# Modulation gradient sums gathered in shared PSUM rows, output column sums behind filler, w_mod rows dealt among the pairs

## The chip, the cores and the metric

The kernel runs on one core of a Trainium2 chip. The metric is the device time of one execution in microseconds (us). Before the change it is 1656.85 us (median of 3 runs, 1653.53 to 1657.62). Engines: PE is TensorE, PEld its weight loads, DVE VectorE, ACT ScalarE, POOL GpSimd, SP SyncE; SPq is SyncE's queue, where the shown time is the issuing of a transfer. The lines of the profile name tiles: pg, pu, pcs, pv and po are the matmul results (in PSUM) of the MLP backward, of the transform ahead of the spectral pairs, of the pairs, of the transform behind them, and of the output. To evacuate such a result is to copy it from PSUM to SBUF (gwo holds evacuated parts of gw2 and gw1, cs01b of pcs). hh and gz are hidden values of the MLP and their gradient, kept in device memory and transposed while they are loaded. A hole is time in which PE waits.

## The reference, cut to what matters

The forward function is a block with a 2-D spectral filter and an MLP, both modulated by six rows made from `silu(c) @ w_mod`. The kernel computes its output and all gradients.

```python
mod = (silu(c) @ w_mod).reshape(1, 6, 1, -1)
sa, ca, ga, sb, cb, gb = rows of mod                  # rows 0..5
h = layernorm(x) * (1 + ca) + sa
x = x + ga * irfft2(rfft2(h) * (w_r + 1j * w_i))      # A: [2048, 1024]
h = layernorm(x) * (1 + cb) + sb
x = x + gb * (gelu(layernorm(h) @ w1 + b1) @ w2 + b2) # w1: [1024, 3584]
out, vjp = jax.vjp(f, x, w_r, w_i, w1, b1, w2, b2, c, w_mod);  grads = vjp(grad_out)
```

The gradient of each modulation row is a sum over 2048 tokens, that is a column sum of a product. From each such row, 1024 x 1024 elements of w_mod's gradient (`out_9`, an outer product with silu(c)) and a part of c's gradient (a product with w_mod) follow.

## The kernel before

Four pieces matter. Column sums are matmuls against all ones, each row of sums with two PSUM banks of its own. A row of w_mod is worked off in eight steps with rings of four buffers. `fill(n)` puts n pieces (16 matmuls of 512 columns each) of w2's gradient (gw2), then of w1's gradient (gw1), between the steps of the spectral backward. A last stage reloads gx1 and A for the sums of row 2 (ga).

```python
def colsum(accs, src, first, last):
    for h in range(2):
        matmul(accs[h], lhsT=ones_bf, rhs=src[:, h * KH:(h + 1) * KH], start=first, stop=last)

for b in range(NB):                       # MLP backward, a block of 512 tokens
    ...                                   # pg matmuls, layer norm backward -> gn3, pru = gn3 * n2u
    for i in range(4):
        colsum(accS, gn3[:, i, :], ...); colsum(accC, pru[:, i, :], ...)
    ...                                   # gx1, folds
store_gmod(accS, 3); store_gmod(accC, 4)  # one row tile, bufs=1: DVE copies, SP stores

def gmod_row(ri, ins):                    # rows in the order 5, 3, 4, 1, 2, 0, all beside gw1
    for jc in range(NDC):                 # 8 steps
        sync.dma_start(wr[jc % 4], w_mod block)
        vector.tensor_scalar(gw[jc % 4], gbf * u[jc])          # product
        gpsimd.dma_start(out_9 block, gw[jc % 4])
        vector.tensor_tensor_reduce(wr[jc % 4], wr * gbf, accum -> gu)

def consume_bwd(i, ...):                  # output part i: unfold, sums, layer norm backward
    tt(tmp, o4, n1, mult)
    for q in range(4): colsum(accCA, tmp[:, q, :], ...)        # directly behind the product
    ...
fill(12); ...; fill(4) per pair; fill(6) per output part
for b in range(NB):                       # sums for ga, near the end
    load gxa <- d_gx1; load ata <- d_A;  tt(gxa, gxa, ata, mult)
    fill(3);  colsum(accGA, gxa, ...)
```

Of the kernel before, what the change touches and what calls it, by code (L numbers as in the profile page):

```python
# [17 lines left out]
P = 128  # L18
# [17 lines left out]
def kernel(  # L36
# [46 lines left out]
    nc.gpsimd.memset(ones_bf[:], 1.0)  # L83
    ident = reg.tile([P, P], BF16, name="ident", tag="ph")
# [91 lines left out]
    def colsum(accs, src, first, last):  # L176
        for h in range(2):
            nc.tensor.matmul(accs[h][:], lhsT=ones_bf[:], rhs=src[:, h * KH:(h + 1) * KH], start=first, stop=last)

    xi = small.tile([P, 32], I32, tag="xi", bufs=1)  # L180
# [201 lines left out]
    def ln_dve(x4, row, i):  # L382
        st = small.tile([P, 4, 2, nc.vector.BN_STATS_DIM], FP32, tag="lnst")
        mv = small.tile([P, 4, 4], FP32, tag="lnmv")
        for q in range(4):
            for h in range(2):
                nc.vector.bn_stats(out=st[:, q, h, :], in_=x4[:, q, h * KH:(h + 1) * KH])
            nc.vector.bn_aggr(out=mv[:, q, 0:2], in_=st[:, q])
        nc.vector.tensor_scalar(out=mv[:, :, 2:3], in0=mv[:, :, 0:1], scalar1=-1.0, scalar2=None, op0=ALU.mult)
        ln_fin(mv[:, :, 1:2], mv[:, :, 2:3], mv[:, :, 3:4], 1.0, row, i)  # L390
# [18 lines left out]
    def spectral_core(fwd, fb, sms, em, css, pt, evac_u, evac_c, evac_v, consume, o4tag, pfs=None, fill=lambda n: None):  # L409
# [4 lines left out]
        def pair(n, par, m):  # L414
            ws = ws2[:, n % 2]
            for x, w in ((0, A_w_r), (1, A_w_i)):
                nc.sync.dma_start(out=ws[:, x, 0, 0:DF], in_=w_plus(w, par, m))
                nc.gpsimd.indirect_dma_start(out=ws[:, x, 1, 0:DF], out_offset=None, in_=w, in_offset=w_idx(par, m))
            cs = css[n % 2]
# [45 lines left out]
            if not fwd:  # L465
                pf = pfs[n % 2]
                nc.sync.dma_start(out=pf.rearrange("p s r w -> p (s r w)"), in_=d_P[n])
                m1 = qb2[:, 0]
                m2 = qb2[:, 1]
                tt(m1[:, :, :, 0:DF], Pv, pf[:, :, :, 0:DF], ALU.mult)  # L470
                tt(m2[:, :, :, 0:DF], Pv, pf[:, :, ::-1, 0:DF], ALU.mult)
                tt(pf[:, 0, :, 0:DF], m1[:, :, 0, 0:DF], m1[:, :, 1, 0:DF], ALU.add)
                tt(pf[:, 1, :, 0:DF], m2[:, :, 0, 0:DF], m2[:, :, 1, 0:DF], ALU.subtract)
                for x, w in ((0, out_2), (1, out_3)):
                    nc.sync.dma_start(out=w_plus(w, par, m), in_=pf[:, x, 0, 0:DF])
                    nc.gpsimd.indirect_dma_start(out=w, out_offset=w_idx(par, m), in_=pf[:, x, 1, 0:DF], in_offset=None)
# [17 lines left out]
        fill(12)  # L494
        for cl in (CE, SE, CO, SO):
            Us[cl] = s_fwd(cl, fb, sms[cl % 2][:, cl // 2], evac_u)
        R = reg.tile([P, 16, 2, PW], BF16, name="R", tag="fr")
# [8 lines left out]
        for cl in range(4):  # L506
            for h in range(2):
                nc.sync.dma_start_transpose(out=gm[:, 2 * cl:2 * cl + 2, h * P:(h + 1) * P],
                                            in_=d_E[:, 0 if fwd else 1, 2 * cl + h, :])
        nc.scalar.mul(out=gm[:, 8:12, :], in_=gm[:, 4:8, :], mul=-1.0)  # L510
        for par in range(2):
            for m in range(4):
# [4 lines left out]
                fill(4)  # L517
# [4 lines left out]
        for i in range(4):  # L522
# [12 lines left out]
            consume(i, o4, ct[:, 1 + i % 2], xts[i % 2])  # L535
            fill(6)
# [7 lines left out]
    def act_copy(out, in_):  # L544
        nc.any.tensor_copy(out=out, in_=in_)  # L545

# [39 lines left out]
    def consume_fwd(i, o4, tmp, x4):  # L586
# [172 lines left out]
    gb1_bf = small.tile([P, NFC], BF16, tag="gb1_bf", bufs=1)  # L759
# [13 lines left out]

    w1Ts = []
# [10 lines left out]
    pru = reg.tile([P, 4, D], BF16, name="pru", tag="uv3")  # L785
    got = reg.tile([P, 6, D], BF16, name="got", tag="ot")
    fbuf2 = reg.tile([P, 4, 4, D], BF16, name="fbuf2", tag="fr")
    accS = [ps_s("accS0"), ps_s("accS1")]
    accC = [ps_d("accC0"), ps_d("accC1")]
    gzn = 0  # L790
    for b in range(NB):
        gn3 = gn3s[b % 2]
        sums = small.tile([P, 2, 4], FP32, tag="sums")
        gzt = []
        for g in range(7):
# [17 lines left out]
        nc.sync.dma_start(out=n3u[:], in_=chunk_rows(d_n3, b))  # L813
        nc.sync.dma_start(out=n2u[:], in_=chunk_rows(d_x1, b))
        norm_act(n2u, n2u, 1, b)
        go4 = got[:, 0:4, :]
        load_tok(go4, grad_out, b)
# [3 lines left out]
        tt(pru[:], gn3[:], n2u[:], ALU.mult)  # L821
        for i in range(4):
            first, last = b == 0 and i == 0, b == 3 and i == 3
            colsum(accS, gn3[:, i, :], first, last)
            colsum(accC, pru[:, i, :], first, last)
        s2c = small.tile([P, 4], FP32, tag="s2c")
        for i in range(4):
            t = 4 * b + i
            nc.vector.tensor_tensor_reduce(out=gn3[:, i, :], in0=gn3[:, i, :], in1=opcb_row, scale=1.0, scalar=0.0,
                                           op0=ALU.mult, op1=ALU.add, accum_out=s2c[:, i:i + 1])  # L830
            ln_bwd(gn3[:, i, :], s2c[:, i:i + 1], n2u[:, i, :], stats[:, 1, 0, t:t + 1], gn3[:, i, :], got[:, 4 + i % 2, :])
        tt(gn3[:], gn3[:], go4, ALU.add)
        nc.gpsimd.dma_start(out=chunk_rows(d_gx1, b), in_=gn3[:])
        tt(n3u[:], gn3[:], bcn(ga_row, 4), ALU.mult)
        fold_tok(n3u, pru)
        fold_d(fbuf2[:, b], n3u[:], pru[:])
    store_gmod([a[0:1, :] for a in accS], 3)
    store_gmod([a[0:1, :] for a in accC], 4)
# [16 lines left out]
    nc.sync.dma_start(out=em2, in_=d_E[:, 0])  # L855
    pf1 = reg.tile([P, 2, 2, PW], BF16, name="pf1", tag="sb")
    pfs = [empf[:, 2048:2048 + 4 * PW].rearrange("p (s r w) -> p s r w", s=2, r=2), pf1[:]]
    otl = reg.tile([P, 2 * NT * P + D], BF16, name="otl", tag="ot")
    sacc = otl[:, 2 * NT * P:2 * NT * P + D]
    hh_s = [hhp[:, 0], hhp[:, 1]] + [otl[:, k * NT * P:(k + 1) * NT * P].rearrange("p (t f) -> p t f", f=P) for k in range(2)]  # L860
    hh_o = [0, 1] * 4 + [2, 3, 0, 1] * 5
# [4 lines left out]
    def consume_bwd(i, o4, tmp, n1):  # L866
# [10 lines left out]
        for q in range(4):  # L877
            colsum(accCA, tmp[:, q, :], i == 0 and q == 0, i == 3 and q == 3)
        s1c = small.tile([P, 4], FP32, tag="s1c")
        for q in range(4):  # L880
# [3 lines left out]
            ln_bwd(o4[:, q, :], s1c[:, q:q + 1], n1[:, q, :], stats[:, 0, 0, t:t + 1], o4[:, q, :], tmp[:, q, :])  # L884
        nc.sync.dma_start(out=n1, in_=chunk_rows(d_gx1, i))
        tt(o4, o4, n1, ALU.add)
        store_tok(out_1, o4, i)
        if i == 3:
            store_gmod([a[0:1, :] for a in accCA], 1)


    u_bfc = small.tile([P, NDC], BF16, tag="u_bfc", bufs=1)
    nc.vector.tensor_copy(out=u_bfc[:], in_=u_col[:])
    u_rt = small.tile([P, NDC], FP32, tag="u_rt", bufs=1)
    nc.vector.tensor_copy(out=u_rt[:], in_=u_bfc[:])
# [12 lines left out]
    GM_ORDER = (5, 3, 4, 1, 2, 0)  # L908
    w1g = {}

# [6 lines left out]
    def gmod_row(ri, ins):  # L917
        r = GM_ORDER[ri]
        wrw, gww, gr = w1g["wr"], w1g["gw"], w1g["gr"]
        with tc.issue_after(ins.ins):  # L920
            gbf = gr[:, ri % 2, :]
            nc.sync.dma_start(out=gbf, in_=d_gmod[r * D:(r + 1) * D].partition_broadcast(P))
            for jc in range(NDC):
                wr, gw = wrw[:, jc % 4, :], gww[:, jc % 4, :]
                nc.sync.dma_start(out=wr, in_=w_mod[jc * P:(jc + 1) * P, r * D:(r + 1) * D])
                nc.vector.tensor_scalar(out=gw, in0=gbf, scalar1=u_rt[:, jc:jc + 1], scalar2=None, op0=ALU.mult)
                nc.gpsimd.dma_start(out=out_9[jc * P:(jc + 1) * P, r * D:(r + 1) * D], in_=gw)
                nc.vector.tensor_tensor_reduce(out=wr, in0=wr, in1=gbf, scale=1.0, scalar=0.0,  # L928
                                               op0=ALU.mult, op1=ALU.add, accum_out=gu[:, r, jc:jc + 1])

    def pieces():
        for fc in range(NFC):
            nc.sync.dma_start_transpose(out=hh_s[hh_o[fc]], in_=d_hh[fc * P:(fc + 1) * P, :])
# [27 lines left out]
        for fg in range(F // 512):  # L961
            if fg < 6:
                ins = gw1_load(fg + 1)
                if fg < 3:
                    gmod_row(fg, ins)
                else:
                    w1g[fg] = ins
# [15 lines left out]
    def fill(n):  # L983
        for _ in range(n):
            next(todo)
        done[0] += n

    spectral_core(False, fbuf2, (smA2, smB2), em2, [css2[:, 0], css2[:, 1]],
                  new_pair_temps(["t0", "t1", "t2", "t3"]), act_copy, act_copy, act_copy, consume_bwd, "fr", pfs, fill)


    accGA = [ps_s("accGA0"), ps_s("accGA1")]
    for b in range(NB):
        gxa = reg.tile([P, 4, D], BF16, name="gxa", tag=f"uv{2 * (b % 2)}")
        ata = reg.tile([P, 4, D], BF16, name="ata", tag=f"uv{2 * (b % 2) + 1}")
        nc.sync.dma_start(out=gxa[:], in_=chunk_rows(d_gx1, b))
        nc.sync.dma_start(out=ata[:], in_=chunk_rows(d_A, b))
        tt(gxa[:], gxa[:], ata[:], ALU.mult)
        fill(3)
        for q in range(4):  # L1000
            colsum(accGA, gxa[:, q, :], b == 0 and q == 0, b == 3 and q == 3)
    store_gmod([a[0:1, :] for a in accGA], 2)
# [8 lines left out]
    assert done[0] <= 56 + 24  # L1011
    fill(56 + 24 - done[0])
    for ri in range(3, 6):
        fill(1)
        gmod_row(ri, w1g[ri])
        fill(7)
    fill(8)
# [41 lines left out]
```

## Time and profile before

| | before |
|---|---|
| median of 3 runs | 1656.85 us |
| profiled span | 1652.7 us |
| PE busy | 1483.8 us, 90% |
| first matmul of the MLP backward (pg) | 866.9 us |
| first matmul of gw2 / first pcs (pairs) / first po (output) | 1076.4 / 1160.5 / 1326.3 us |
| PE's last matmul | 1638.3 us |

These two lines of the page of the kernel before show where PE falls short: busy us of each engine, and PE's busy tenths in 40 slices of 41.3 us.

```profile
PE 1483.8 (90%) x6826; PEld 679.9 (41%) x6826; DVE 1074.8 (65%) x1546; ACT 734.7 (44%) x989; POOL 360.3 (22%) x421
...
PE   3788999999598987999979999979999997889796
```

In the backward half, the 27th slice (1074 to 1116 us, the start of gw2) falls short, and so do five of the seven from the 34th on (1363 us). The next two lines are from PE's timeline at the start of gw2. In the brackets stand the idle time ahead of the matmuls and what ended it:

```profile
1082.41 1.39 PE L899 MATMUL gw2acc<-gB,hhsA 128*128 128x512 bf16 x5 [3.28 <-DVE gB L168]
...
1088.99 1.01 PE L178 MATMUL accS<-gn3b,ones_bf 128*128 128x512 bf16 x2 [5.19 <-DVE gn3b L772]
```

PE first waits for gB (the upstream gradient in natural order, scaled by DVE), then the last block's sums wait for VectorE. The later holes are shown in the prediction.

### The profile page before, as it was taken

The numbers are of one execution on the slowest core, as the hardware profiler recorded it, in microseconds if no ns is written. First come the engines' busy times: TensorE is split into PE (matmuls) and PEld (weight loads), VectorE is DVE, ScalarE is ACT, GpSimd is POOL, SyncE is SP. The second block draws the span as 40 slices with busy tenths as digits, with TensorE's granted clock in tenths as the row PEclk, the third lists the DMA queues.
The fourth block names the chain that finished last, engine by engine and source line by source line (L and its number), as shares of the span: only waits on it lengthen the run. The fifth ranks groups of instructions, "written<-read, shape, count | busy, mean of one in ns | idle before, by whom it ended". The sixth has DMA issues, their size and how long they took to land.

```text
span 1652.7 us, 18418 instructions
## 1 busy us (share of the span) xinstructions
PE 1483.8 (90%) x6826; PEld 679.9 (41%) x6826; DVE 1074.8 (65%) x1546; ACT 734.7 (44%) x989; POOL 360.3 (22%) x421
## 2 busy tenths in 40 slices
PE   3788999999598987999979999979999997889796
PEld 2333555443233433444434444434444453334342
DVE  3586386786677887786511777884564587788633
ACT  2676555858666565665311334334213353312111
POOL 3350161111011221222110000320233101323222
PEclk9899999999799998999989999989999999989898
DMA  9953568797555676699984245546675639798997
GB/s 300 245 170 100 104 192 254 241 254 197 186 157 184 202 233 206 214 278 280 246 257 116 65 173 178 172 154 168 152 188 159 195 104 204 256 291 264 248 237 151
DMA packets 380279, 329.52 MB, mean 199 GB/s; under 512 B 230167, under 2 KB 321303, under 8 KB 380062
## 3 DMA queue, kind: packets, MB, share of 16 engines
q1 hardware_dynamic: 344302, 210.86, 49.7%
q0 software_dynamic: 33792, 114.36, 21.2%
q10 hardware_dynamic: 2096, 3.15, 0.7%
q8 instruction: 53, 0.87, 0.2%
q14 instruction: 36, 0.29, 0.1%
HBM read 166.77 MB, written 108.05 MB: 166 GB/s over the span
## 4 chain that ended last, share of the span: by engine, by line
PE 33%; DMA 10%; DVE 9%; issue 7%; ACT 3%; POOL 2%; SPq 0%; POOLq 0%; ACTq 0%; DVEq 0%
PE gw2acc L899 10%; PE pg L805 5%; PE pbo L706 5%; PE pz L670 3%; PE gw1acc L972 2%; DVE got L767 2%; PE pu L403 2%; PE pcs L427 2%; PE pv L489 2%; DMA d_gz<-gt 2%; DVE ct L168 2%; DMA xt<-d_gx 1%; DVE gn3a L772 1%; DMA wrw<-in_w_mod_dram 1%; DMA gB<-in_grad_out_dram,xu 1%
## 5 line engine op out<-in xcount | busy, mean ns | idle before, releaser
L616 PE MATMUL pp<-gBoT,wt 128*128 128x512 bf16 x896 | 206.4, 386 | 1.2 <-DVE pho L623 1.2
L972 PE MATMUL gw1acc<-gzh,n3n 128*128 128x512 bf16 x896 | 197.9, 382 | 6.2 <-ACT gwo L904 6.0
L805 PE MATMUL pg<-w1T,gzr 128*128 128x512 bf16 x896 | 196.6, 379 | 0.4
L670 PEld LDWEIGHTS <-w 128*128 128x128 bf16 x896 | 89.8, 100 | 124.0 <-issue 24.2
L972 PEld LDWEIGHTS <-n3n 128*128 128x128 bf16 x896 | 88.1, 98 | 111.3 <-issue 7.8
L616 PEld LDWEIGHTS <-wt 128*128 128x128 bf16 x896 | 89.3, 100 | 108.2 <-issue 9.1
L899 PE MATMUL gw2acc<-gB,hhsA 128*128 128x512 bf16 x576 | 130.2, 383 | 3.3 <-DVE gB L168 3.3
L805 PEld LDWEIGHTS <-gzr 128*128 128x128 bf16 x896 | 87.5, 98 | 106.9 <-issue 1.5
L168 DVE TENSOR_TENSOR gt<-gt,gt 128x2048 bf16<-128x2048 bf16 x84 | 102.0, 1223 | 24.3 <-ACT gt L678 23.0
L976 ACT CAST gwo<-gw1acc 128x512 bf16<-128x512 f32 x53 | 30.9, 585 | 180.0 <-PE gw1acc L972 138.3
L670 PE MATMUL pz<-n3Ta,w 128*128 128x512 bf16 x448 | 103.6, 393 | 5.8 <-ACT gt L673 5.8
L670 PE MATMUL pz<-n3Tb,w 128*128 128x512 bf16 x448 | 102.3, 388 | 4.2 <-ACT gt L673 4.2
L706 PEld LDWEIGHTS <-hhA 128*128 128x128 bf16 x608 | 60.1, 100 | 94.3 <-issue 21.6
L673 ACT ACTIVATE gt<-pz,b_col 128x512 bf16<-128x512 f32 x112 | 71.5, 684 | 35.7 <-PE pz L670 33.9
L899 PEld LDWEIGHTS <-hhsA 128*128 128x128 bf16 x576 | 57.3, 100 | 71.4 <-issue 5.2
L904 ACT CAST gwo<-gw2acc 128x512 bf16<-128x512 f32 x50 | 29.1, 583 | 127.2 <-PE gw2acc L899 126.1
L674 ACT ACTIVATE gt<-gt 128x2048 bf16<-128x2048 bf16 x28 | 53.3, 1908 | 64.3 <-DMA d_gz<-gt 64.0
L168 DVE TENSOR_TENSOR ct<-ct 128x2048 bf16<-128x2048 bf16 x64 | 75.8, 1219 | 5.3 <-DMA d_n<-ct 4.3
L677 ACT ACTIVATE gt<-gt 128x2048 bf16<-128x2048 bf16 x28 | 53.5, 1911 | 52.9 <-DVE gt L168 52.9
L899 PE MATMUL gw2acc<-gB,otl 128*128 128x512 bf16 x320 | 71.5, 380 | 0.0
L545 DVE CAST cs01b<-pcs 128x512 bf16<-128x512 f32 x16 | 11.1, 693 | 82.5 <-PE pcs L427 82.5
L928 DVE CUSTOM_DVE_ANT_0 wrw<-wrw,gr 128x1024 bf16<-128x1024 bf16 x48 | 58.0, 1215 | 5.0 <-DMA wrw<-in_w_mod_dram 4.9
(273 smaller groups left out, 2523.5 us busy)
## 6 DMA issues: line engine op xcount, KB each, us to landing
d_gz<-gt POOLq DMA_DIRECT2D x28, 512.0 KB, 4.3
gzr<-d_gz SPq DMA_DIRECT2D x28, 512.0 KB
wrw<-in_w_mod_dram SPq DMA_DIRECT2D x48, 256.0 KB
out_dram<-otl POOLq DMA_DIRECT2D x48, 256.0 KB, 5.1
wblk<-in_w_mod_dram SPq DMA_DIRECT2D x11, 1024.0 KB
d_ph<-pho POOLq DMA_DIRECT2D x21, 512.0 KB, 4.6
d_hh<-hhA POOLq DMA_DIRECT2D x19, 512.0 KB, 4.3
w2sD<-in_B_w_dram SPq DMA_DIRECT2D x14, 512.0 KB
```

The lines of the kernel that those rows point to most:

```text
L168: nc.vector.tensor_tensor(out=out, in0=a, in1=b, op=op)
L403: nc.tensor.matmul(pu[:], lhsT=fb[:, i, cl, c8 * P:(c8 + 1) * P], rhs=sm[:, i, :], start=(i == 0), stop=(i == 3))
L616: nc.tensor.matmul(pp[:], lhsT=wt[:, fg % 2, cch, k * P:(k + 1) * P], rhs=gBoT[j][:, cch, :], start=(cch == 0), stop=(cch == NDC - 1))
L670: nc.tensor.matmul(pz[:], lhsT=w1s[g][:, cch, k * P:(k + 1) * P], rhs=n3T[:, cch, :], start=(cch == 0), stop=(cch == NDC - 1))
L673: nc.scalar.activation(out=zb[:, k, :], in_=pz[:], func=ACT.Identity, bias=b1_col[:, fc:fc + 1], scale=1.0)
L674: nc.scalar.activation(out=av, in_=zb, func=ACT.Square)
L677: nc.scalar.activation(out=sg, in_=bv, func=ACT.Sigmoid, scale=2.0 * GK)
L706: nc.tensor.matmul(pbs[i][:], lhsT=hh[:, k, i * P:(i + 1) * P], rhs=wp[:, k, :], start=False, stop=(g == 6 and k == 3))
L805: nc.tensor.matmul(pgs[i][:], lhsT=gzt[g][:, k, i * P:(i + 1) * P], rhs=w1Ts[g][:, k, h * KH:(h + 1) * KH], start=(g == 0 and k == 0), sto ...
L899: nc.tensor.matmul(acc[:], lhsT=hh_s[hh_o[fc]][:, t, :], rhs=gBs[t // 4][:, t % 4, h * KH:(h + 1) * KH], start=(t == 0), stop=(t == NT - 1))
L928: nc.vector.tensor_tensor_reduce(out=wr, in0=wr, in1=gbf, scale=1.0, scalar=0.0, op0=ALU.mult, op1=ALU.add, accum_out=gu[:, r, jc:jc + 1])
L972: nc.tensor.matmul(acc[:], lhsT=n3ns[t // 4][:, t % 4, cch * P:(cch + 1) * P], rhs=gz2[t // 8][:, t % 8, :], start=(t == 0), stop=(t == NT ...
```

## The change

The intent is to empty the output stage and the end of waits on VectorE and of traffic. (1) The sums for rows 3, 4 and 2 share one pair of PSUM banks: a one-column selector as stationary operand puts them in rows 0, 32 and 64. Those for row 2 are made in the MLP backward from A (tile `au`), so the last stage goes. (2) The last block's sums stand behind 6 pieces of gw2. (3) In the output stage, the column sums stand behind 6 to 8 pieces. (4) Row 5 of w_mod is dealt in the MLP backward, three steps per block, and rows 3 and 4 beside the pairs, with one buffer for weights and one for products. (5) The first eight blocks of hh are transposed into other buffers (`hht`, made of those of the MLP backward), two ahead. (6) A pair's weights are loaded one pair ahead. (7) The pcs of the pairs are all evacuated by ScalarE; before, VectorE and ScalarE took 16 each.

```diff
+    sel = const.tile([P, P + 64], BF16)           # zeros, column 64 ones
-    def colsum(accs, src, first, last):
+    def colsum(accs, src, first, last, lhs=None): # lhsT = sel[:, 64 - 32 * lhs:192 - 32 * lhs]
...
+        nc.sync.dma_start(out=n3u, in_=d_n3[b]); ...      # loads of the block moved to its start
-            colsum(accS, gn3[:, i, :], ...); colsum(accC, pru[:, i, :], ...)
+        if b < NB - 1: sums3(b, gn3, pru)                 # acc3, PSUM rows 0 and 32
+        nc.sync.dma_start(out=au, in_=d_A[b]); tt(au, g2, au, mult)
+        if b < NB - 1:
+            sums3_ga(b, au)                               # acc3, PSUM row 64
+            for _ in range(3): next(early, None)          # w_mod row 5
-    store_gmod(accS, 3); store_gmod(accC, 4)
...
-    hh_o = [0, 1] * 4 + [2, 3, 0, 1] * 5
+    hh_o = [4, 5, 6, 7] * 2 + [0, 1] + [2, 0, 1] * 6      # 4..7: hht; hh loads two blocks ahead
-        fill(12)
+    fill(6); sums3(3, gn3s[1], pru); fill(10)
+    def mid_bwd():                                        # behind half of s_fwd
+        sums3_ga(3, au)
+        for k in range(3): store_gmod(acc3 row 32 * k, (3, 4, 2)[k])
+    rows34 = [gmod_steps(r, gmy[:, 0:1], gmy[:, 1:2], sacc) for r in (3, 4)]
+    def beside_bwd(n):
+        for k in range(4):
+            fill(1)
+            if k < (0, 2, 2, 2, 2, 2, 3, 3)[n]: next(rows34[side[0] // NDC]); ...
-    spectral_core(..., act_copy, act_copy, act_copy, ...) # nc.any: VectorE or ScalarE
+    spectral_core(..., act_copy, s_copy, act_copy, ...)   # pcs: ScalarE alone
...
         tt(tmp, o4, n1, ALU.mult)
-        for q in range(4): colsum(accCA, tmp[:, q, :], ...)
+        ...                                               # layer norm backward, stores
+        fill((6, 6, 8, 8)[i])
+        for q in range(4): colsum(accCA, tmp[:, q, :], ...)
+        fill(2)
-    accGA stage (4 blocks: two loads, product, fill(3), sums)
-    rows 5, 3, 4, 1, 2, 0 in the gw1 stage
+    for r in (2, 1, 0): gmod_row(r, w1g["ins"]); fill(8)
```

## The prediction

> **What bounds the kernel now.** I read the page's slices first: TensorE (PE) is busy 90% of a 1652.7 us span, nearly 100% in most slices, so only the slices that fall short can be shortened. The order of instructions of the two kernels, compared engine by engine, then says where to look: up to the MLP backward PE runs the same matmuls with a few fillers moved, and PE executes exactly as many matmuls in all. So I cut the backward half into stretches by the windows view (columns: stretch, length, busy us and instructions of PE, PE weight loads, VectorE (DVE), ScalarE (ACT), GpSimd; granted PE clock; DMA share; GB/s).
>
> ```profile
> 866.50:1076.40 209.90, 207.82 (x951) 92.49 (x950) 135.22 (x186) 69.58 (x106) 26.62 (x23) 1.00 0.44 143
> 1076.40:1102.70 26.30, 17.82 (x70) 7.20 (x69) 20.77 (x31) 6.49 (x8) 7.73 (x5) 0.81 0.49 168
> 1102.70:1326.00 223.30, 223.30 (x1035) 106.27 (x1034) 122.05 (x159) 77.88 (x125) 49.34 (x52) 1.00 0.65 169
> ...
> 1340.00:1433.00 93.00, 75.16 (x366) 37.33 (x365) 74.43 (x103) 37.09 (x50) 20.96 (x21) 0.93 0.76 189
> 1433.00:1469.90 36.90, 36.90 (x172) 16.67 (x171) 30.19 (x48) 10.06 (x14) 9.89 (x16) 1.00 0.96 306
> 1469.90:1545.00 75.10, 56.23 (x241) 24.29 (x240) 61.49 (x92) 12.14 (x17) 21.10 (x34) 0.86 0.95 262
> ```
>
> MLP backward (first line) and the spectral pairs (third) keep PE full; the loss is at the start of the w2 gradient (second) and in the spectral output and after it (the rest). The timeline of PE in the last stretches names the holes, in brackets with what ended them:
>
> ```profile
> 1388.39 0.58 PE L972 MATMUL gw1acc<-gzh,n3n 128*128 128x512 bf16 x1 [6.02 <-ACT gwo L904]
> ...
> 1421.10 3.43 PE L178 MATMUL accCA<-ct,ones_bf 128*128 128x512 bf16 x8 [4.12 <-DVE ct L168]
> 1428.22 1.87 PE L531 MATMUL po<-gm,V 128*128 128x256 bf16 x8 [3.69 <-ACT ct L534]
> ...
> 1477.60 2.72 PE L178 MATMUL accCA<-ct,ones_bf 128*128 128x512 bf16 x6 [7.69 <-DVE ct L168]
> ...
> 1537.19 3.57 PE L178 MATMUL accGA<-gxa,ones_bf 128*128 128x512 bf16 x8 [10.27 <-DVE gxa L168]
> ```
>
> **The ceiling.** From 866.5 to PE's last matmul (1638.3) are 771.8 us. A steady 512-column matmul takes 0.2158 us (139 of gw2acc in 30.00 us). The stretch holds 3078 of them (896 pg, 896 gw2, 896 gw1, 256 pu and pv, 134 sums and pa), 664.2 us; 128 pcs at 0.216 are 27.6 and 128 po at 0.109 are 14.0. Sum 705.8, so 66 us are lost: about 45 in plain holes of 0.7 us and more, the rest mostly in the slow clock after them. No part of the change can win more than these 66.
>
> **What the Trainium skill says.** "TensorE: Matmul & The Clock Gate", Part 1, What's actually happening: a window of about 3.4 us without work halves the PE clock. The trace agrees: 0.50 in 1535-1540, and the eight sums after the 10.27 us hole took 3.57 us where the next eight took 1.89. The same page, Step-by-step, says that a matmul streams N columns, whatever its stationary operand: so a sum through the one-column selector costs what one through all ones costs (8 in 1.89 us here). "DMA: Bandwidth & Descriptors", Issuing engines are not separate DMA queues: all queues share 16 engines. The trace agrees: a 256 KB gw2 store landed in 3.7 us (median) at 1160-1330, w_mod row stores in 5.1 where the DMA was full. "Perfetto Trace Analysis", What "DMA-bound" means, counts the issuing sequencer itself as something that can bind; here four gz transposes held SyncE's (SP) queue 30.57 us from 1369.44, while ACT waited 10.84 and 7.02 us for an x load.
>
> **The change part by part.**
>
> 1. *Sums for ga in the MLP backward.* Its 32 matmuls stay; the stage near the end goes, with 8 MB of loads (4 MB remain, read in the backward) and its four DVE products (2.3 us each; they return as the au products). PE waited 0.91 + 10.27 us there, and about 2.5 us went to the slow clock: gain 13.5. In the MLP backward DVE has 6.6 us free per block and needs 2.3 more: hidden.
>
> 2. *Last block's sums behind 6 pieces (96 matmuls, 20.7 us).* Before, PE waited 3.28 us for gB, then 5.19 for gn3b; the stretch lost 26.3 - 70 x 0.2158 = 11.2. The second hole is covered. But hh is now transposed into buffers that are freed only in the last h pass, among the four gB loads, and an au load is there too: 2.5 MB more in 1060-1080, where the DMA already moved 390 GB/s: 6.4 us at that rate. gB's hole grows from 3.3 to some 9, and pru then comes 22.9 us after the last gB against PE's 20.4. I put 11 us again: gain 0.
>
> 3. *Three sums in shared PSUM rows.* They hold both banks that the first pcs of the pairs needs, until three rows are copied out, each copy waiting for the store of the one before (row has one buffer). Between these stores SP has two hh transposes (2.1-3.3 us each) and three smi transposes (24.85 us for 16). From the end of pu's first half I count: 5 smi 7, hh 5, store 3, copy 1.3, 3 smi behind it, store 3, copy 1.3: 21 us; PE arrives after 15.5. New wait: 5 us.
>
> 4. *w_mod rows.* One row (5) runs in the idle DVE at 874-915; 8 serial stores of some 4 us each fit its 41 us. Rows 3 and 4, 16 steps of 0.48 + 1.22 us, go into the pairs, where DVE has 122 of 223 us; the casts of pcs (16 x 0.69) move to ACT. Work fits. But each step now has one buffer for the product and one for the weights, and 7 of the 16 products stand in DVE's order in a row between pairs 5 and 6, each behind the previous one's store (0.5 + 0.6 issue + 4 to 4.5 landing, about 5.5). That is some 44-49 us from pair 5's start to pair 6's, where 31 were needed before: DVE 13-18 us late. The last pair had 5.2 us of slack before pv and part of the lag is taken up by an earlier wait for an evacuation that DVE does late: new wait about 6.
>
> 5. *Column sums of the output behind filler, more filler per part (8 to 10 pieces against 6), rows 5, 3, 4 gone from there.* Before, 1340-1545 held 366 + 172 + 241 = 779 matmuls, 96 of them short po: 205 - 683 x 0.2158 - 96 x 0.109 = 47 us lost; less the 13.5 of part 1, some 33 here. DVE has 31 us of work per part against 33-40 of PE: the four accCA waits (13.7 us and slow clock) go. But w2's gradient now ends after the first part instead of the second, so the gz transposes (about 7 us each) start beside the x loads, and x loads stand behind them on SP: I expect 4 us for the second gz tile, 2 for a sum, 5 for evacuations that ACT holds behind an x load, 3 later, 3 of slow clock: 17. Gain about 16.
>
> 6. *Loads of the pairs one pair ahead:* the pairs had no hole; worth nothing.
>
> **Sum.** Losses afterwards: 5 (MLP backward, as before) + 11 + 5 + 6 + 17 = 44, against 66: 22 us. Span 866.5 + 705.8 + 44 + 14.4 (the tail after PE's last matmul, whose order of transposes and row stores is unchanged) = 1630.7. Runs were 4 us over the span before, in the median: 1634.
>
> **Rivals.** *All waits hidden:* the fillers look placed with care, and fewer row transfers late in the kernel may shorten transposes and x loads. If parts 2 to 4 cost only 8 and part 5 only 10, the losses are 23 and the time 1613. For it: DMA share 0.95 to 1.06 from 1433 on, relieved by 12.6 MB of rows and 4 MB of loads. *Serial row steps and SP's queue win:* DVE held at single buffers delays hh loads, R and evacuations, PE loses 20 in the pairs and 30 in the output: time 1660. For it: SP waits in order, and row loads now stand between hh loads. Against it: hh is loaded two chunks ahead, about 12 us of slack. *DMA hidden anyway:* the removed transfers never held PE except through the 10.27 us hole, so only part 1 counts: 1643.
>
> **Range and chances.** The centre is 1634; the parts 2 to 5 are each unsure by 5 to 8 us, together some 13, and placed fillers make the better side a little more likely than my count: I say 1632, 8 in 10 within 1610 to 1651. Over 2% faster means under 1623.7, which needs 10 us more than my count: 0.33. Slower by over 2% (1690) needs the loss to double: 0.02.
>
> **What would show it.** accGA's hole gone; a longer gB wait at the first gw2acc (7 to 13 us); the first pcs waiting for the copies of acc3 (about 5); DVE products waiting for their own stores before pair 6, then pv waiting for R (about 6); accCA waits gone; gw1 waiting for gz or for an evacuation behind an x load. Wrong if pcs and pv start without a wait (then nearer 1615), or if the pairs starve for hh (then over 1650).

## The result, and the profile after

The changed kernel takes 1627.6 us (median of 4 runs, 1623.9 to 1629.95), the kernel before in the same rounds 1655.46 us (1653.53 to 1657.62). The ratio is 0.9829, 95% interval 0.9806 to 0.9853. Ratios here are the mean time of one kernel's runs over that of the other's runs of the same rounds, so not quite the ratio of the medians quoted. The same lines of the page:

```profile
PE 1477.3 (91%) x6826; PEld 680.1 (42%) x6826; DVE 1069.9 (66%) x1539; ACT 739.5 (45%) x996; POOL 361.9 (22%) x423
...
PE   3689999999588987999979999979999989999997
```

From the 34th slice on all but the last are full now. The 27th still falls short, and the 33rd (1302 to 1343 us) has become so. PE's timeline names the holes that stand in the backward half instead:

```profile
1090.13 1.86 PE L947 MATMUL gw2acc<-gB,hht 128*128 128x512 bf16 x4 [6.85 <-DVE gB L171]
1094.12 19.80 PE L947 MATMUL gw2acc<-gB,hht 128*128 128x512 bf16 x84 [2.13 <-DVE gB L171]
1184.75 2.45 PE L436 MATMUL pcs<-empf,U 128*128 128x256 bf16 x8 [3.49 <-DVE row L176]
1327.63 0.59 PE L947 MATMUL gw2acc<-gB,otl 128*128 128x512 bf16 x1 [4.62 <-DVE gwo L952]
1331.05 3.57 PE L436 MATMUL pcs<-empf,U 128*128 128x256 bf16 x8 [2.83 <-ACT cs01b L559]
...
1433.97 0.60 PE L543 MATMUL po<-gm,V 128*128 128x256 bf16 x4 [2.90 <-ACT ct L546]
...
1589.84 28.87 PE L1013 MATMUL gw1acc<-gzh,n3n 128*128 128x512 bf16 x120 [3.44 <-DMA gzh<-d_gz]
```

Of the holes before, those ahead of accS, accCA and accGA are gone. The wait for gB is longer, the first pcs waits for a copied row, and near the last pair gw2 and pcs wait for evacuations.

To see where the time went, I cut the backward half at the first matmul of each stage and took away the work, with the prediction's costs (0.2158 us for a 512-column matmul, 0.216 for a pcs, 0.109 for a po; for example MLP backward after: 972 x 0.2158 = 209.8 of 220.6 us). In the traces of ref_after, row_tiles, two_products, gb_queue and hh_old_slots 134 of the 6826 matmul records are missing; there the matmuls of the program are counted. What is left is lost, holes and slow clock together:

| us lost | MLP backward | gw2 start to first pcs | pairs | output to PE's last matmul | sum | tail after it |
|---|---|---|---|---|---|---|
| before | 4.9 | 11.6 | 0.1 | 49.0 | 65.6 | 14.4 |
| predicted | 5 | 11 + 5 | 6 | 17 | 44 | 14.4 |
| after, first trace | 10.8 | 15.3 | 12.2 | 13.8 | 52.2 | 9.4 |
| after, second trace (ref_after) | 8.5 | 16.9 | 14.0 | 7.0 | 46.5 | 12.0 |

The output wins 35 to 42 us, and the three stretches ahead of it give back 22 to 23. So the expected gain was there, and more than half of it turned into new waits. A further 3 to 6 us come from ahead of the cut: pg starts at 860.8 and 863.8 us in the two traces, at 866.9 before.

### The profile page after: what moved, and what is told of

Its sections match the earlier page's. It is cut to its first block, busy times and chain, and to the rows that moved or that the text cites. A ratio compares the mean times of both kernels' runs of the same rounds, so it can differ in the third digit from the quotient of the medians.

```text
span 1628.1 us, 18389 instructions
## 1 busy us (share of the span) xinstructions
PE 1477.3 (91%) x6826; PEld 680.1 (42%) x6826; DVE 1069.9 (66%) x1539; ACT 739.5 (45%) x996; POOL 361.9 (22%) x423
## 5 line engine op out<-in xcount | busy, mean ns | idle before, releaser
L947 PE MATMUL gw2acc<-gB,hhsA 128*128 128x512 bf16 x448 | 100.8, 381 | 0.0
L947 PE MATMUL gw2acc<-gB,hht 128*128 128x512 bf16 x256 | 58.3, 390 | 9.0 <-DVE gB L171 9.0
L947 PEld LDWEIGHTS <-hhsA 128*128 128x128 bf16 x448 | 44.5, 99 | 51.5 <-issue 0.2
L497 PE MATMUL pv<-smi,R 128*128 128x512 bf16 x256 | 57.9, 380 | 0.7 <-DVE R L171 0.7
L221 PE MATMUL pm<-wblk,u_b 128*128 128x512 bf16 x96 | 27.8, 438 | 30.4 <-DMA wblk<-in_w_mod_dram 30.4
```

The lines of the kernel that those rows point to most:

```text
L497: nc.tensor.matmul(pv[:], lhsT=R[:, cl * 4 + m, :, :].rearrange("p x w -> p (x w)")[:, base:base + 255:2], rhs=smi[:, cl // 2, m, :], star ...
L947: nc.tensor.matmul(acc[:], lhsT=hh_s[hh_o[fc]][:, t, :], rhs=gBs[t // 4][:, t % 4, h * KH:(h + 1) * KH], start=(t == 0), stop=(t == NT - 1))
```

## The experiments

Each kernel below is the changed kernel with the edit named; each was timed in rounds with the kernel before, and all gave correct results. Only gb_queue, row_tiles and two_products ran in the same rounds as ref_after. Between the sets of rounds the median of the kernel before varied from 1653.63 to 1655.89 us, so a difference of medians to ref_after is good to some 2 us at best for the others, and the ratios are given beside it where they say something else. A trace is one execution, so in the table of losses a difference of 2 or 3 us may be chance, as the two traces of the same kernel show.

| run | median us | ratio to before (95%) | lost in MLP / gw2 start / pairs / output | tail |
|---|---|---|---|---|
| ref_after | 1629.57 | 0.9842 (0.9811-0.9872) | 8.5 / 16.9 / 14.0 / 7.0 | 12.0 |
| row_tiles | 1622.63 | 0.9801 (0.9777-0.9825) | 12.6 / 12.1 / 10.8 / 7.0 | 9.3 |
| two_products | 1623.61 | 0.9816 (0.9786-0.9847) | 8.4 / 16.3 / 14.5 / 7.2 | 9.7 |
| early_steps | 1621.85 | 0.9811 (0.9775-0.9848) | 8.8 / 14.9 / 9.9 / 7.6 | 13.0 |
| gb_queue | 1647.80 | 0.9956 (0.9927-0.9984) | 18.1 / 22.0 / 18.9 / 7.2 | 9.4 |
| gb_first | 1632.70 | 0.9872 (0.9826-0.9918) | 11.5 / 16.5 / 19.0 / 7.5 | 12.2 |
| hh_px1 | 1638.60 | 0.9897 (0.9870-0.9924) | 8.8 / 22.5 / 11.5 / 10.8 | 15.1 |
| ca_first | 1638.33 | 0.9932 (0.9890-0.9975) | 10.7 / 15.5 / 13.0 / 20.0 | 8.4 |
| ga_end | 1635.01 | 0.9911 (0.9866-0.9957) | 6.1 / 14.1 / 6.4 / 27.4 | 13.3 |
| fwd_loads | 1632.48 | 0.9866 (0.9836-0.9896) | 9.1 / 16.8 / 16.8 / 7.5 | 11.6 |
| all_mended | 1638.39 | 0.9896 (0.9868-0.9924) | 8.8 / 22.4 / 8.8 / 10.7 | 16.4 |
| hh_old_slots | 1636.15 | 0.9899 (0.9870-0.9928) | 10.8 / 25.5 / 12.6 / 8.9 | 13.9 |

### The yardstick

> The changed kernel, unaltered, as the yardstick for the runs beside it. Expected ratio to the kernel before 0.980 to 0.986 (it was 0.9829). It also tells how far two traces of the same kernel differ in the forward half: the MLP backward's first matmul came at 860.8 us in the first trace of the changed kernel and at 866.9 us before; if that gap belongs to the change, it comes within 1.5 us of 860.8 again; if it is chance, it may lie anywhere from 859 to 867.

The ratio came out at 0.9842, and pg starts at 863.8 us, 3 us later than in the first trace. The hole of 3.44 us ahead of gw1 in the first trace is not there in the second: it was chance. The holes at gB (0.51, 6.54, 2.06 us), at the first pcs (3.81) and at the last pair (6.39, 3.01) came again.

### The wait ahead of the first pcs: a tile for each row

```diff
-    row = small.tile([1, D], BF16, tag="gmrow", bufs=1)       # one tile for the three rows
+    row = the same for row 3; pt_rows[:, k * D:(k + 1) * D] (an idle pair buffer) for rows 4 and 2
```

> One edit: the three rows of sums that are taken from PSUM ahead of the pairs get a row tile each (two of them in a pair buffer that is idle then) instead of sharing one, so no row's copy waits for the store of the row before it. Theory: the hole of 3.49 us in front of the first pcs, which the trace puts down to the last row copy, goes, 3 to 5 us faster. Rival: the pcs are held by the transposes for em2/smi or by the copies' PSUM reads themselves; the hole stays at 2 to 4 us and the time moves less than 1.5 us.

VectorE's copies of the three rows from PSUM, in its timeline, with the shared tile (ref_after):

```profile
1182.85 0.68 DVE L176 CAST row<-acc3a 1x512 bf16<-1x512 f32 x1 [12.36 <-DMA d_gmod<-row]
...
1186.27 0.69 DVE L176 CAST row<-acc3a 1x512 bf16<-1x512 f32 x1 [2.14 <-DMA d_gmod<-row]
```

And with a tile each (row_tiles), where PE's first pcs follows without a bracket:

```profile
1172.59 0.67 DVE L177 CAST row<-acc3b 1x512 bf16<-1x512 f32 x1
1173.29 0.68 DVE L177 CAST Pt<-acc3a 1x512 bf16<-1x512 f32 x1
...
1185.81 1.89 PE L437 MATMUL pcs<-empf,U 128*128 128x256 bf16 x8
```

A store of 2 KB held the next copy for 12.36 us, since it stood in SyncE's queue behind transposes: five for smi (6.94 us) and two for hh (5.47) were issued before it, at 1180.30. With three tiles the copies follow one another and PE does not wait; its first eight pcs take 1.89 us in place of 3.60. The loss in the stretch falls from 16.9 to 12.1 us, and the median falls by 6.9 us. The theory holds. The difference in time beyond those 5 us is not accounted for, and the two intervals just overlap.

### The pairs: double the product buffer

```diff
-    gmod_steps(r, gmy[:, 0:1], gmy[:, 1:2], sacc)     # one product buffer
+    gmod_steps(r, gmy[:, 0:1], gmy[:, 1:3], sacc)     # two; otl grows into room that its tag has
```

> One edit: the w_mod rows dealt beside the pairs get two product buffers in place of one (1024 columns that the tile's tag has to spare). Theory: six products in a row waited 1.4 to 4.4 us each for the store of the one before, 17.5 us of VectorE in front of pair 6's sums, and with two buffers these waits fall below 8 us in all, the holes of 4.62 us (gw2) and 2.83 us (pcs) with the slow clock after them go: 5 to 9 us faster. Rival 1: the chain runs through GpSimd's queue and the x gather (ScalarE waited 16.1 us for xt); stores still queue one behind the other, and the gain is 0 to 4 us. Rival 2: the single weight buffer takes the place as the wait: gain under 2 us.

In ref_after the products of the w_mod steps wait for their own stores, one after the other, and the gather of xt (x for the output part) stands behind these stores in GpSimd's queue. Lines of the timelines of DVE, POOL and ACT:

```profile
1316.09 0.49 DVE L798 TENSOR_SCALAR otl<-otl,u_rt 128x1024 bf16<-128x1024 bf16 x1 [3.23 <-DMA out_dram<-otl]
...
1325.32 0.54 POOL L799 DMA_DIRECT2D out_dram<-otl  x1 [4.19 <-DVE otl L798]
1326.16 1.01 POOL L130 DMA_INDIRECT xt<-in_A_x_dram,xu  x1 [0.30 <-issue]
...
1329.57 3.50 ACT L398 ACTIVATE xt<-xt,stats 128x1024 bf16<-128x1024 bf16 x3 [18.09 <-DMA xt<-in_A_x_dram,xu]
```

With two product buffers, ACT's and PE's lines are these:

```profile
1326.56 3.50 ACT L398 ACTIVATE xt<-xt,stats 128x1024 bf16<-128x1024 bf16 x3 [16.55 <-DMA xt<-in_A_x_dram,xu]
...
1330.58 0.59 PE L947 MATMUL gw2acc<-gB,otl 128*128 128x512 bf16 x1 [5.87 <-ACT gwo L952]
1333.65 3.57 PE L436 MATMUL pcs<-empf,U 128*128 128x256 bf16 x8 [2.48 <-ACT cs01b L559]
```

DVE's waits for stores fell from 20.9 us (6.04, 2.73, 3.23, 1.96, 4.25, 2.68) to 9.9 (4.43, 0.79, 3.56, 1.15), and pair 6's sums began at 1320.40 instead of 1328.10. PE's holes stayed all the same, 8.4 us against 9.4, and the pairs lose 14.5 us against 14.0. So the first rival is right in what it forecast: with VectorE freed, PE is held by ACT, which sits on xt with the evacuations of gw2 and pcs behind it. In ref_after itself VectorE was late as well. It evacuated gw2 only at 1331.83, behind the last product (1327.70) and pair 6's sums, and this ended PE's first hole (6.39 us, put down to DVE); ACT's evacuation of a pcs at 1335.53, behind xt, ended the second (3.01). The median is 6 us lower, but no stretch of the trace shows it as the buffer's doing.

### The pairs: fewer steps ahead of the gather

```diff
-            if k < (0, 2, 2, 2, 2, 2, 3, 3)[n]:
+            if k < (0, 3, 3, 3, 3, 2, 1, 1)[n]:
```

> One edit: the sixteen w_mod steps beside pairs 0 to 7 are dealt 0,3,3,3,3,2,1,1 instead of 0,2,2,2,2,2,3,3. With two product buffers VectorE had finished pair 6's sums early, yet the hole stayed (5.9 and 2.5 us), because ScalarE sat 16.6 us on xt, whose gather stands behind the products' stores in GpSimd's queue. Theory: with fewer stores ahead of the gather (3 instead of 6 or 7), the gather is issued 8 us or more earlier, ScalarE's wait on xt falls below 10 us and the holes at pairs 6 and 7 (6.4 and 3.0 us) shrink below 3 us in all: 4 to 9 us faster. Rival: pairs 1 to 4 become the bottleneck by VectorE's waits for stores and weights; new holes of 5 us or more appear there and nothing is gained.

ACT's wait for xt, and PE's holes from 1240 to 1365 us:

```profile
1322.13 3.51 ACT L398 ACTIVATE xt<-xt,stats 128x1024 bf16<-128x1024 bf16 x3 [6.13 <-DMA xt<-in_A_x_dram,xu]
...
1260.87 3.30 PE L436 MATMUL pcs<-empf,U 128*128 128x256 bf16 x8 [3.74 <-ACT cs01b L559]
1299.47 12.25 PE L497 MATMUL pv<-smi,R 128*128 128x512 bf16 x56 [2.70 <-ACT V L556]
```

ACT waits 6.13 us in place of 18.09, and the holes at the last pair are gone, as the theory says. Two smaller ones have come in earlier pairs, 6.4 us against 9.4, so the rival has a share too. The pairs lose 9.9 us against 14.0. The median is 7.7 us lower (5 by the ratio), but the interval is too wide to tell it from the changed kernel by the time alone; the verdict rests on the waits. The other traces bear it out: the three kernels with this dealing (this one, all_mended and hh_old_slots) show no hole at gw2's evacuation there, and nine of the ten traces with the old dealing do, 4.6 to 11.8 us (not ga_end). The dealing also shortens VectorE's waits for its stores, so the run doesn't say that ACT's wait alone made the holes. And the second hole, a pcs that waits for ACT, may owe something to part 7 of the change, which put all these evacuations on ACT; no run undid that.

### The wait for gB: another queue

```diff
-        load_tok(gb_t, grad_out, b)
+        load_tok(gb_t, grad_out, b, nc.gpsimd)        # plain half of the load on GpSimd's queue
```

The first suspicion came from SyncE's queue. In the changed kernel it issues, between the gB loads, the new transposes of hh and a load of A:

```profile
1067.15 11.76 SPq L972 DMA_TRANSPOSE hht<-d_hh  x1
1079.01 0.52 SPq L878 DMA_DIRECT2D au<-d_A  x1
1079.62 1.84 SPq L127 DMA_DIRECT2D gB<-in_grad_out_dram  x1
1081.52 5.91 SPq L972 DMA_TRANSPOSE hht<-d_hh  x1
1087.53 0.53 SPq L127 DMA_DIRECT2D gB<-in_grad_out_dram  x1
```

> One edit: the plain loads of the four gB tiles (upstream gradient in natural order) are issued from GpSimd's queue instead of SyncE's. Theory: the new hht transposes sit in front of them in SyncE's queue (one held it 11.76 us), so gB tiles 2 and 3 are asked for only at 1079.6 and 1087.5 us; with the loads elsewhere the holes of 6.85 and 2.13 us in front of the first gw2 sums shrink to 3.5 us or less in all and the kernel is 5 to 9 us faster than the changed kernel. Rival 1: the loads are slow because the transposes fill the DMA engines; then the holes stay above 7 us and the time moves less than 1.5 us. Rival 2: VectorE's chain to the sums is next in line and the hole only moves to the sums or to the first stage after; gain 0 to 3 us.

This failed. The holes grew to 22.8 us in all (9.63, 2.51, 9.22 and 1.47):

```profile
1090.84 1.86 PE L947 MATMUL gw2acc<-gB,hht 128*128 128x512 bf16 x4 [9.63 <-DVE gB L171]
...
1106.31 1.86 PE L947 MATMUL gw2acc<-gB,hht 128*128 128x512 bf16 x4 [9.22 <-DVE gB L171]
```

The edit did not do what it was meant to: GpSimd's queue asked for the four loads at 1063.26, 1066.81, 1073.54 and 1088.19 us, the last no earlier than before (1087.53). And the gathers that bring the other half of each gB tile, all issued by 1074.6 in the changed kernel, stood behind these loads in the same queue and were issued until 1092.9. So the run is no clean test of SyncE's order. Meanwhile SyncE issued two transposes one after the other from 1079.70 to 1107.34 us, and the last two gB tiles arrived in that time. These rows of the windows view are for the kernel before and for this run (columns: stretch, length, busy us of PE, PEld, DVE, ACT, POOL; granted clock, DMA share, GB/s):

```profile
1065.00:1075.00 10.00, 10.00 (x48) 4.53 (x47) 5.16 (x3) 0.84 (x3) 8.17 (x7) 1.00 1.03 390
1075.00:1085.00 10.00, 5.52 (x25) 2.24 (x23) 8.36 (x7) 1.91 (x6) 8.24 (x5) 0.92 1.04 388
```

```profile
1070.00:1080.00 10.00, 9.95 (x47) 4.54 (x47) 0.00 (x0) 1.17 (x3) 2.69 (x3) 1.00 1.04 137
1090.00:1100.00 10.00, 3.73 (x8) 1.13 (x9) 5.30 (x4) 0.00 (x0) 6.09 (x3) 0.50 1.19 168
```

The DMA engines are as busy in both, but with transposes in flight they move 137 to 168 GB/s (217 in the ten us between) instead of 390. The pairs got worse too, by the hole of 10.68 us at the last pair.

### The wait for gB: transposes behind the loads

```diff
+            if fc in (1, 2, 3):
+                with tc.issue_after(gb_in.ins):       # the last gB load
                     hh_in[0] = nc.sync.dma_start_transpose(out=hh_s[hh_o[fc]], in_=d_hh[...])
```

> One edit: the second to fourth transposes of hh wait, in SyncE's queue, until the plain loads of all four gB tiles have been issued; one transpose (it serves the first two gw2 sums) stays ahead. The run with the gB loads on GpSimd's queue made the holes longer (9.6, 2.5, 9.2, 1.5 us), which speaks against the queue position alone and for the transposes sharing the DMA engines with the loads: 137 to 217 GB/s where both were in flight, against 380 to 410 GB/s in the kernel before. Theory: with the transposes behind the loads, the holes of 6.5 and 2.1 us in front of gw2 shrink to 3 us or less in all; the kernel is 4 to 9 us faster than the changed kernel (ratio to before 0.978 to 0.982). Rival: the hole only moves to the second block, which then waits for its late transpose: within 2 us of the changed kernel.

The holes were 0.69, 4.83 and 2.61 us, 8.1 in all, against 9.1: next to nothing won. The loads were all issued by 1075.6, but two transposes followed at once (18.09 us in the queue), and the third gB tile still reached VectorE only at 1090.6. This is the cleaner test of the order: three of the loads were asked for at 1069.91, 1072.58 and 1075.18 us, against 1065.67, 1079.62 and 1087.53 in the changed kernel, and PE waited nearly as long. An order of issue did not keep the transfers apart here. The median is 3 us above ref_after (5 by the ratio) with a wide spread (1620.83 to 1642.62), and this trace has a hole of 11.76 us at the last pair, which varies from trace to trace.

### The wait for gB: transposes long before

```diff
-    au in px1; w_mod row 5 early in ph and sb; hh_o = [4, 5, 6, 7] * 2 + [0, 1] + [2, 0, 1] * 6
+    au in two halves in ph and sb (n3u for the last block); row 5 at the end with 2, 1, 0
+    hh_o = [0, 1, 4] + [0, 1, 2] * 8 + [0]            # 0 and 1 (px1) are free all through the MLP backward
```

> The buffers of the MLP backward's new work are changed about: the tile for A (for the sums of gx1 times A) is held in two halves in the buffers that the early w_mod row had (the last block's in n3u), that row (5) goes to the end of the gw1 stage with 2, 1 and 0, and the first two blocks of hh get back the buffer that is free through the whole MLP backward, so that their transposes are done long before gw2; the third waits for the gB loads to be issued. Theory: the holes in front of gw2 are the transposes sharing the DMA engines with the gB loads in the last 20 us of the MLP backward; without them these holes fall from 8.5 to 9.5 us to 4 us or less, as in the kernel before, and the loss in the first sums (2.7 us in some traces) goes: 4 to 9 us faster, less 0 to 4 us for the eight steps more at the end. Rival: gB's own 4 MB and the gx1 and A traffic are enough to hold it; holes of 6 us or more stay, no gain.

Two blocks were transposed early, but the third's single transpose was issued at 1072.80, right behind the last gB load, and the traffic fell with it:

```profile
1070.00:1080.00 10.00, 10.00 (x48) 4.51 (x47) 4.59 (x2) 0.00 (x0) 7.87 (x6) 1.00 1.10 294
1080.00:1090.00 10.00, 4.44 (x21) 1.92 (x20) 1.72 (x1) 2.75 (x8) 3.52 (x1) 0.87 1.16 145
```

The holes were 6.19 and 2.61 us. A new one of 7.00 us came at 1140 us, where a later transpose (into a buffer that the MLP backward frees late) was waited for, and the eight steps more at the end cost 3.1 us of waits for gz and a longer tail. The run is slower than the changed kernel.

### Undone: column sums directly behind their product

```diff
-        fill((6, 6, 8, 8)[i]);  colsum(accCA, ...) x4;  fill(2)
+        colsum(accCA, ...) x4 directly behind tt(tmp, ...);  fill((8, 8, 10, 10)[i])
```

> Undoes one part: in the output stage the column sums for row 1 stand directly behind their product again, with all filler after them (8, 8, 10, 10 pieces). Theory of the prediction: the sums then wait for VectorE as in the kernel before (holes of 0.7, 1.2, 4.1 and 7.7 us there), so 8 to 13 us slower than the changed kernel. Rival: those waits came from the w_mod rows that VectorE worked on in that stage and that are now dealt elsewhere; then under 4 us slower.

```profile
1424.91 3.57 PE L181 MATMUL accCA<-ct,ones_bf 128*128 128x512 bf16 x8 [5.59 <-DVE ct L171]
1464.69 3.36 PE L181 MATMUL accCA<-ct,ones_bf 128*128 128x512 bf16 x8 [3.28 <-DVE ct L171]
```

The sums wait for VectorE again: 0.67 us ahead of the first part's, then as shown, and 3.10 ahead of the last part's, 12.6 us in all, nearly the 13.7 of the kernel before. They run slowly after two of the waits (3.57 and 3.36 us for eight instead of 1.89). The output loses 20.0 us against 7.0, and the median rises by 8.8 us (15 by the ratios, 0.9932 against 0.9842). So the filler ahead of the sums is worth some 6 to 15 us here (6 and 13 by the two traces of the changed kernel) even without the w_mod rows in that stage; the rival (under 4 us) falls.

### Undone: sums for ga at the end

```diff
-        au load, product and sums3_ga in the MLP backward
+        accGA stage at the end as before (12 pieces); fill((6, 4, 4, 2)[i]) in the output to pay for them
```

> Undoes one part: the sums of gx1 times A for row 2 are taken at the end from reloaded tiles, as in the kernel before, with three pieces of filler ahead of each block's; the MLP backward keeps the shared rows for the two other sums only, and the output stage has 12 pieces fewer to hide its own waits. Theory of the prediction: the hole of about 10 us before the first of these sums comes back, and the part's work at the start of gw2 goes (1 to 3 us better there): 6 to 12 us slower than the changed kernel. Rival: the hole was due to the w_mod rows' loads and stores in that stage; then within 3 us.

The median rose by 5.4 us and the ratio from 0.984 to 0.991, which is some 11 us; the two intervals just overlap. The stretches show both sides. The output loses 27.4 us against 7.0; the MLP backward wins 2.4 to 4.7, and the pairs 6 to 8. But the expected hole of 10 us is not there:

```profile
1505.27 1.89 PE L181 MATMUL accGA<-gxa,ones_bf 128*128 128x512 bf16 x8 [1.72 <-DVE gxa L171]
1516.12 1.89 PE L181 MATMUL accGA<-gxa,ones_bf 128*128 128x512 bf16 x8 [2.71 <-DVE gxa L171]
```

The sums for ga wait 4.8 us in all; 4.0 us stand ahead of accCA, which has less filler, 8.2 ahead of po, and 3.9 at gz. So the large hole before did not come from these sums alone. What it came from is read from the trace of before and not tested by a run: there the gxa loads of 1515.62 and 1520.52 us stood among w_mod loads in SyncE's queue, while all DMA moved 395 to 410 GB/s (1520 to 1535 us). The holes at gB (2.02, 4.94 and 2.18 us, 9.1 in all) stay without any load of A: the load of A is not what makes them. Why the pairs lose less here is open; two rows instead of three are copied ahead of them.

### Undone: loads of the forward pairs one pair ahead

```diff
+                if fwd: pair_load(par * 4 + m)         # at the start of the pair, as before
                 pair(par * 4 + m, par, m)
-                if par * 4 + m < 7: pair_load(par * 4 + m + 1)
+                if not fwd and par * 4 + m < 7: pair_load(par * 4 + m + 1)
```

> Undoes one part, in the forward half only: each pair's two weight blocks are asked for at the start of that pair again, not one pair ahead. Nine traces of kernels with the changed forward half reach the MLP backward's first matmul at 858.1 to 864.0 us (mean 862.3); the one trace of the kernel before reached it at 866.9 us. Theory: the earlier loads are worth these 4 to 5 us; without them the first matmul of the MLP backward comes at 866 us or later and the kernel is 3 to 6 us slower than the changed kernel. Rival: the gap is chance in one trace of before, or the rest of the changed order; it comes at 860 to 864.5 us again and the time does not move.

pg starts at 863.2 us, in the middle of the other traces with the changed forward half (858.1 to 864.0). So the loads are not what makes the forward half shorter. The median is 2.9 us above ref_after, within the spread; its trace has a hole of 11.06 us at the last pair. There is only one trace of the kernel before, and what makes its 866.9 us remains open.

### Mends together

> Four edits together: the buffers as in the run with the early hh transposes, a tile for each of the three rows, two product buffers, and the w_mod steps dealt 0,3,3,3,3,2,1,1. If the gains add up (row tiles 7 us by the ratio, early steps 5, early hh 4 to 9, product buffers 0 to 4): 1605 to 1615 us, ratio to before 0.970 to 0.976. If they only trade one wait for another: 1615 to 1625 us.

The edits of hh_px1, row_tiles, two_products and early_steps together give 1638.39 us. The pairs lose 8.8 us, fewest but for ga_end, and no row copy is waited for. But the buffers of hh_px1 bring its losses along: 6.03 and 2.61 us at gB, 7.63 at the late transpose, 3.8 at gz, and a tail of 16.4 us. The gains do not add up.

```diff
-    hht slots 4..7 of tags t2, t3, two blocks ahead
+    slots 4, 5 = the halves of gzr[2]; hh_o = [4, 5] * 4 + [0, 1] + [2, 0, 1] * 6
+    blocks 2 to 7 are asked for only when the block two before has been used
```

This last edit stands on the changed kernel's own buffers, with the row tiles, two product buffers and earlier steps.

> The last mend, on the changed kernel's own buffers: the row tiles, two product buffers and the earlier dealing as measured, and the first eight blocks of hh take turns in two slots of the gz ring. The first slot is idle from the third block on, so its transpose is done some 50 us before gw2; the second comes free at about 1056 us; no further transpose is asked for until the first gw2 sums are done. In the run before, one single transpose next to the gB loads still pulled the DMA engines to 21 to 117 GB/s (380 to 420 without) and left holes of 6.2 and 2.6 us; leaving it open whether that one transpose is enough. Theory: with none between 1066 and 1085 us the holes in front of gw2 are 4 us or less in all (3.3 in the kernel before), and the kernel takes 1602 to 1614 us (ratio to before 0.968 to 0.975). Rival: with no transpose there the loads still come late (holes of 6 us or more), or the third block's transpose, asked for only when the first is done, is waited for (a hole of 3 us or more): 1612 to 1622 us.

```profile
1089.76 1.87 PE L947 MATMUL gw2acc<-gB,gzr 128*128 128x512 bf16 x4 [4.72 <-DVE gB L171]
1094.23 20.36 PE L947 MATMUL gw2acc<-gB,gzr 128*128 128x512 bf16 x82 [2.61 <-DVE gB L171]
1143.70 4.02 PE L947 MATMUL gw2acc<-gB,gzr 128*128 128x512 bf16 x9 [11.84 <-DMA gzr<-d_hh]
```

With no transpose issued from 1069 to 1100 us the wait for gB is 7.3 us, shorter than 9.1 but not the 3.3 of before. One transpose still stood in the queue ahead of three of the loads (1060.97, 7.54 us); all DMA moved 186 GB/s from 1070 to 1075 us and 383 to 385, as in the kernel before, only from 1075 to 1085. Later a block that was asked for late is waited for 11.84 us. The rival is right about the waits, and 1636.15 us is no gain at all, above even its range.

The fastest were early_steps and row_tiles, one small edit each; both beat the kernel before, and their medians lie 7 to 8 us under that of ref_after (early_steps only 5 by the ratio). The row tiles, two buffers and earlier steps without any change to hh were never run together.

## Why the prediction was right or wrong

The time was right: 1632.0 predicted, 1627.6 and (second set of runs) 1629.57 measured, within 1610 to 1651, and within 2% as held likeliest. The mechanism, waits traded for new waits, was right in kind. The sum was closer than its terms, and part of that was luck, as told below.

- **Part 1 (13.5 us gained, hidden in the MLP backward).** The stage at the end and its hole are gone. "Hidden" was wrong: the MLP backward loses 8.5 to 10.8 us, not 5. VectorE had the time, but in each of the first three blocks the sums stand directly behind the au product, and PE waits 0.97 us for it, 2.9 in all; without the part (ga_end) these waits are gone and the stretch loses 6.1. Undone, the part costs 5.4 us by the median and some 11 by the ratio, not 13.5. In ga_end, where rows 5, 3 and 4 of w_mod have left that stage, the hole is short (4.8 us in all for these sums); that they made it long is likely, not tested.
- **Part 2 (gain 0; gB's hole 9 us, 11 lost in all).** Right in size: 8.98 and 9.1 us of holes in the two traces, and no wait of the sums. The cause, transposes of hh among the gB loads, is supported by the throughput in gb_queue, hh_px1 and hh_old_slots; the load of A, which I named as well, is not needed for the hole, as ga_end shows. No run brought back the 3.3 us of before, so how much belongs to the transposes is not settled.
- **Part 3 (5 us at the first pcs).** A sum through the selector costs what was said: eight start 0.215 us apart (950.97 to 952.69 us). The wait was right in kind and nearly in size: 3.49 and 3.81 us and the slow clock after them. row_tiles confirms the chain of copy and store, and the queue held just the transposes that I had counted. Eight of the ten traces with one shared tile have this hole (2.7 to 4.4 us; not ga_end, which copies two rows, nor hh_px1), none of the three with a tile for each row.
- **Part 4 (6 us at the last pair).** The mis-sized term: the pairs lose 12 to 14 us. The prediction's step "DVE products waiting for their own stores before pair 6, then pv waiting for R" failed in its second half. The products waited as said (20.9 us in ref_after), yet pv did not wait. Evacuations did, on two engines: gw2's on VectorE, late behind the products, ended the first hole, and a pcs's on ACT, held 16 to 18 us by xt, whose gather stood behind those stores in GpSimd's queue, ended the second. Freeing VectorE alone (two_products) leaves the holes, since ACT is late too; early_steps, which shortens both engines' waits, closes them. Beside the holes (7.5 and 9.4 us) some 4.7 us are lost, most of it in the slow clock after them. The Trainium skill, "TensorE: Matmul & The Clock Gate", Part 1, What's actually happening, puts the throttled clock at half; the trace agrees: 3.57 us for eight pcs against 1.89.
- **Part 5 (17 us left in the output).** Too much: 13.8 and 7.0 us. None of the sums waits. Evacuations that ACT does late, behind a step of the layer norm, cost 2.9 us rather than 5 and 3, and the wait for gz came in one trace of two. ca_first shows that filler ahead of the sums carries some 6 to 15 us.
- **Part 6 (pair loads ahead: nothing).** fwd_loads agrees. But the prediction left the forward half at 866.5 us, and all traces of the new one are 3 to 9 us shorter.
- **The tail (14.4, unchanged).** It was 9.4 and 12.0 us, and 8.4 to 16.4 in the variants. The last evacuation's wait for a store before it, 8.73 us before, was 3.89 and 6.46.

Against 44 us the losses were 52 and 46; a forward half and a tail shorter by 5 to 11 us together, neither of which was foreseen, made up for it. That was luck. (One reading of the prediction is loose: the 5.1 us for w_mod row stores "where the DMA was full" is the median of all 48 on the page; from 1400 to 1560 us it is 5.5.) Of the rivals, "serial row steps and SP's queue win" named some of the right waits, the evacuations, but they took 12 to 14 us in the pairs, not 20, and nothing in the output.

## What to carry to other kernels

Work moved off the last, slow stage into full ones takes its buffers and queue places along: here most of the work itself was hidden (the sums behind the au product excepted), and the waits came from a shared 2 KB row tile, stores ahead of a gather in one queue, and transposes moved next to urgent loads. When an engine waits, look at what stands ahead of its data in the issuing queue before doubling the buffer at the wait that looks busiest. And be wary of transposes in a stretch in which plain loads are awaited: the traffic fell with them here, and changing the order of issue did not help. That moving them away wins time is not shown, as each run that tried it brought a new wait of 7 to 12 us.

## What the Trainium skill lacked or had wrong

- The Trainium skill, "DMA: Bandwidth & Descriptors", Latency and other measured facts, gives an effective 261 GB/s for a DMA transpose, and about 350 to 400 where contiguous. It doesn't say what transposes do to plain loads beside them. Here all DMA together fell from 388-390 GB/s (DMA share 1.03-1.04) to 137-217 GB/s (share 1.04-1.19) with transposes of 512 KB in flight, and to 145 GB/s with a single one.
- The same page, Issuing engines are not separate DMA queues, calls the time on the issuing sequencer usually small relative to the transfer. The transfers do share the engines, as it says. But one transpose held SyncE's sequencer for 11.76 us, and a row store of 2 KB kept its buffer 12.36 us behind such transposes.
- "PSUM — Partial Sum Buffer", Specifications (TRN2), warns that a non-contiguous access pattern slows matmuls significantly; I found no page that gives the cost. Here eight matmuls of 256 columns whose PSUM output has a step of 2 (pcs) take 1.89 us, as much as eight with 512 columns, while eight po of 256 columns side by side took 1.04. No run changes the step alone.
